# Scratch blocks in DRAM with rows of 4352 bytes in place of contiguous rows

## The chip, the core and the metric

The kernel runs on one core of a Trainium2 chip. A core has a matrix engine (PE, with its weight loads shown as PEld), a vector engine (DVE), a scalar engine (ACT), a general engine (POOL) and a synchronisation engine (SP), each with its own instruction queue, and 16 DMA engines that move data between DRAM and the on-chip memory SBUF. A DMA is issued by SP (queue q1 of the profile) or by POOL (queue q0), is cut into packets, and is spread over the DMA engines; it has landed when the last of them is done. The metric is device time in microseconds of one execution.

## The reference

Two computations share the layer-normalised input `xn` and are summed with the input. In one, a recurrent attention, segments of 32 rows are worked one after the other; each takes 8 rows of memory from the segment before:

```
for s in range(64):                       # 2048 rows, 32 per segment
    h = concat([mem, xn[32*s : 32*s+32]]) # 40 rows x 1024
    q, k, v = h @ Wq, h @ Wk, h @ Wv      # 32 heads of 128, so 4096 columns each
    p = softmax(mask(q @ k.T * scale))
    o = (p @ v) @ Wo                      # 4096 -> 1024
    mem = o[:8];  out[32*s : 32*s+32] = o[8:]
```

In the other, the two rows with the largest router value `xn @ w_r` go through one gated expert (1024 to 3584 and back), are scaled by the sigmoid of that value, and are added to their rows. The result is `x + attention + (xn + expert update)`. All tensors are bf16.

## The kernel before

**Granules.** The weights Wq, Wk, Wv and Wo, 32 MB in all, are cut into 64 granules of 128 partitions x 2048 elements, 512 KB each. Granules 0 to 47 are a slice of 128 rows by half of the columns of Wq, Wk or Wv, so a row is 4096 bytes and rows in the input lie 8192 bytes apart. Granules 48 to 63 are two slices of 128 rows of Wo, 2048 bytes a row. All 64 are needed in each of the 64 segments, in order, and not all fit in SBUF: 43 are loaded once and stay (`wres`), 21 are *streamed* (1, 4, 7, 10, 13, 16, 19, 22 and so on to 62, about one in three). Granule 10 is kept whole in on-chip accumulator memory and copied from there (`kept_piece`), and of granule 19 a quarter is kept, so that 1536 of its 2048 elements a row are streamed.

**The ring.** A streamed granule goes into one of `N_SLOT = 5` SBUF slots (`wstream`, the tile `g`). `fetch` (lines 304 to 314) issues the load on SP's queue. It is called from `after(s, g)` when a streamed granule has been used, so the next load waits for a slot whose readers on PE are done. In the first segment the load reads the inputs (line 311). From the second on it reads a scratch block in DRAM, `wsc[g]` (line 313):

```
wsc = {g: dram.tile([P, 1536 if g == KEPT_PART else 2048], ...)}      # line 103
nc.sync.dma_start(out=t[:, 0:n], in_=wsc[g][:, 0:n])                  # line 313
```

`copy_block` (lines 333 to 337) fills each `wsc` block once, during the first segment, by a DMA from the input to the scratch block on POOL's queue, in granule order, one with every second granule that is used. A block is contiguous: 128 rows of 4096 bytes one behind the other (3072 bytes in the block of granule 19). It belongs to the scratch pool `dram`, in which also `ql_d` lies, a store for queries, keys and values of the rows that a segment does not need at once.

**The segment.** Six passes multiply the segment's transposed rows with the granules (lines 614 and 597: Q, K, Q, K, V, V halves), with the attention's steps hooked in between; then Wo's 16 granules are multiplied (line 662), and the new memory goes back into the next segment's operand. Other DMAs of a segment are small ones on POOL's queue: rows of x, the stores to `ql_d` and from it, and the output rows.

**The end.** After the last segment the expert's weights are loaded (`fetch_moe`, lines 354 and 357, tiles `MW`), straight from the inputs: gate and up in rows of 3584 bytes, 7168 bytes apart, down in rows of 2048 bytes.

The order of the instructions is the program's own; no scheduler moves them.

Of the kernel before, what the change touches and what calls it, by code (L numbers as in the profile page):

```python
# [8 lines left out]
BF16 = mybir.dt.bfloat16  # L9
# [10 lines left out]
KEPT_WHOLE = 10  # L20
KEPT_PART = 19
# [6 lines left out]
def kernel(  # L28
# [16 lines left out]
    nc = tc.nc  # L45
    P = 128
# [27 lines left out]
    streamed = sorted(set(((2 * i + 1) * NG) // (2 * n_str) for i in range(n_str)))  # L74
    resident = [g for g in range(NG) if g not in streamed]

    def granule_dram(g):
        if g < 48:
            p, kc = divmod(g, KC)
            mat, half = PHASES[p]  # L80
            return Wqkv[mat][kc * P:(kc + 1) * P, 2048 * half:2048 * (half + 1)]
        w = g - 48
        return Wo2[2 * w * P:(2 * w + 2) * P, :].rearrange("(hh e) d -> e hh d", hh=2)

    def granule_out(t, g):
        return t[:, :] if g < 48 else t.rearrange("p (hh d) -> p hh d", hh=2)
# [3 lines left out]
    dram = ctx.enter_context(tc.tile_pool(name="dram", bufs=1, space=DRAM))  # L90
# [9 lines left out]


    ql_d = [dram.tile([4, P, 512], BF16, name=f"ql_d{t}") for t in range(NT)]
    wsc = {g: dram.tile([P, 1536 if g == KEPT_PART else 2048], BF16, name=f"wsc{g}") for g in streamed if g != KEPT_WHOLE}
    r_d = dram.tile([1, S], BF16, name="r_d")

    res_tiles = {}
# [55 lines left out]
    for s in range(4):  # L162
        nc.vector.tensor_copy(out=SELM[:, s, :, 0:XM],
                              in_=IDENT[:, 32 * s:32 * s + XM].unsqueeze(1).to_broadcast([P, 4, XM]))
        nc.vector.tensor_copy(out=SELL[:, s, :, :],
                              in_=IDENT.rearrange("p (s c) -> p s c", c=32)[:, :, XM:SEG])
# [166 lines left out]
    def copy_block(g):  # L333
        n = kept_at.get(g, 2048)
        if n:
            src = granule_dram(g)
            nc.gpsimd.dma_start(out=granule_out(wsc[g], g) if g >= 48 else wsc[g][:, :], in_=src if g >= 48 else src[:, 0:n])

    to_copy = list(streamed)
    flow += [(s, g) for s in range(NSEG) for g in streamed]  # L340
# [70 lines left out]
    def after(s, g):  # L411

        if s == 0:
            if g in side:
                side[g]()
            if g % 2 == 1 and g >= 8 and to_copy:
                copy_block(to_copy.pop(0))
            if n_x_left and g % 2 == 1:
                load_x(n_x_left.pop(0))
            while todo_res and todo_res[0] <= g + 2 * 64 // n_str + 8 and (todo_res[0] < resident[-10] or g >= 2 * NT + 12):  # L420
                load_resident(todo_res.pop(0))
        if g in streamed:
            fetch()
        if s == NSEG - 1:
            if g in resident:
                free_homes.append(g)
            if not flow:
                fetch_moe()
# [39 lines left out]
    for s in range(NSEG):  # L468
# [132 lines left out]
        for p, (mat, half) in enumerate(PHASES):  # L601
# [8 lines left out]
            for kc in range(KC):  # L610
                g = 8 * p + kc
# [16 lines left out]
            if mat < 2:  # L628
# [3 lines left out]
                if PSl is not None:  # L632
# [3 lines left out]
                    for jq in range(4):  # L636
                        nc.gpsimd.dma_start(out=ql_d[left[mat]][:, 32 * jq + c0:32 * jq + c0 + 8, :],  # L637
                                            in_=XBl[32 * jq:32 * jq + 32, :])
# [195 lines left out]
```

## Time and profile before

| | |
|---|---|
| median of 3 runs | 2194.16 us (2191.17 to 2204.95) |
| the profiled execution's own time | 2187.56 us |
| its span, first to last instruction | 2186.0 us |
| PE busy | 1710.7 us, 78% |
| DMA moved | 754.63 MB, mean 345 GB/s |
| `g<-wsc`: reads of a scratch block | 1197 of 512 KB and 63 of 384 KB |
| PE waiting for `g<-wsc` at line 614 | 174.0 us in 289 waits |
| mean granted PE clock | 0.94 |

The profile is one execution, taken by the hardware profiler. A row of the windows view has a stretch, the busy time of each engine (with the number of instructions), the granted PE clock, the busy share of the 16 DMA engines and the rate. [...] "To landing" is the time from the issue of a DMA to its last byte, and holds the waiting behind earlier DMAs of the same queue. The chain that ended last goes back from the last instruction to what released it, and so on. The trace holds one record for each DMA packet with its queue, size, start and duration, but not its engine.

### The profile page before, as it was taken

What the parts mean: (1) busy time and instruction counts of PE and PEld (TensorE: products, weight loads), DVE (VectorE), ACT (ScalarE), POOL (GpSimd) and SP (SyncE); (2) the same over time, 40 slices, a digit from 0 to 9 for tenths busy, and PEclk for the clock granted to TensorE, in tenths of its full rate; (3) what the DMA queues carried; (4) which work ended last, traced back from release to release, by engine and by line L of the source; (5) the groups of instructions that cost most, each with busy time, mean ns of one, the idle gap of its engine ahead of it and who ended that gap; (6) DMA issues with size and microseconds to landing.
All of it is one profiled execution on the core that took longest, in us unless ns stands there. A gap on an engine that the chain in (4) does not pass through costs nothing.

```text
span 2186.0 us, 82770 instructions
## 1 busy us (share of the span) xinstructions
PE 1710.7 (78%) x36135; PEld 907.9 (42%) x36135; DVE 718.1 (33%) x2335; ACT 670.5 (31%) x1865; POOL 641.5 (29%) x1218
## 2 busy tenths in 40 slices
PE   3257788888888788878888788888888888888854
PEld 1124444444444444444444444444444444444433
DVE  5623332332333233332333233233333333333320
ACT  0013233332333333333333333333333333333320
POOL 4223233232323322332323322332332233232120
PEclk8669999999999999999999999999999999999986
DMA  9999899998999999999999989899998999999996
GB/s 362 374 263 350 320 355 327 358 364 297 360 345 370 344 350 369 333 358 322 369 350 361 325 329 375 324 349 335 362 351 330 380 343 349 338 360 346 378 396 241
DMA packets 245244, 754.63 MB, mean 345 GB/s; under 512 B 49872, under 2 KB 56176, under 8 KB 244880
## 3 DMA queue, kind: packets, MB, share of 16 engines
q1 hardware_dynamic: 203440, 712.46, 87.5%
q0 software_dynamic: 41440, 36.86, 5.8%
q8 instruction: 283, 4.64, 0.9%
q14 instruction: 81, 0.66, 0.1%
HBM read 736.39 MB, written 22.95 MB: 347 GB/s over the span
## 4 chain that ended last, share of the span: by engine, by line
DMA 53%; PE 30%; issue 6%; ACT 4%; POOL 4%; DVE 2%; SPq 0%; ACTq 0%; DVEq 0%; POOLq 0%
DMA g<-wsc 36%; PE PSm L614 10%; DMA ql_d<-XBl 8%; PE WO L662 8%; DMA XL<-in_A_x_dram 3%; PE PSl L597 3%; PE WL L662 3%; POOL ql_d L637 2%; PE BO L550 1%; DMA LX<-ql_d 1%; POOL XL L272 1%; ACT VM L642 1%; DMA XP<-in_A_x_dram 1%; PE BT L251 1%; PE BT L484 1%
## 5 line engine op out<-in xcount | busy, mean ns | idle before, releaser
L614 PE MATMUL PSm<-wres,ST 128*32 128x512 bf16 x8192 | 683.6, 389 | 5.4 <-DVE ST L266 5.4
L614 PEld LDWEIGHTS <-ST 128*32 128x32 bf16 x12288 | 323.9, 96 | 595.3 <-issue 262.5
L614 PE MATMUL PSm<-g,ST 128*32 128x512 bf16 x4096 | 413.3, 390 | 190.6 <-DMA g<-wsc 174.0
L630 ACT CAST XB<-PSm 128x512 bf16<-128x512 f32 x256 | 150.0, 586 | 429.5 <-PE PSm L614 427.4
L637 POOL DMA_DIRECT2D ql_d<-XBl x256 | 152.4, 601 | 383.9 <-ACT XBl L634 369.8
L662 PE MATMUL WO<-wres,OT 128*32 128x256 bf16 x5632 | 254.1, 288 | 7.8 <-issue 7.6
L662 PEld LDWEIGHTS <-OT 128*32 128x32 bf16 x8192 | 206.7, 101 | 88.0 <-issue 56.9
L238 POOL DMA_DIRECT2D X<-in_A_x_dram x256 | 132.4, 525 | 375.3 <-PE WO L648 276.8
L707 POOL DMA_DIRECT2D out_dram<-OB x256 | 128.0, 507 | 383.9 <-DVE OB L705 378.3
L597 PE MATMUL PSl<-wres,STL 128*32 128x512 bf16 x2048 | 194.8, 395 | 1.7 <-ACT VL L644 1.7
L662 PE MATMUL WO<-g,OT 128*32 128x256 bf16 x2560 | 138.1, 292 | 33.2 <-DMA g<-wsc 21.7
L642 ACT CAST VM<-PSm 128x512 bf16<-128x512 f32 x128 | 76.9, 601 | 282.0 <-PE PSm L614 235.6
L557 ACT CAST OT<-BO 128x128 bf16<-128x128 f32 x256 | 67.9, 265 | 240.1 <-PE BT L552 236.6
L557 DVE CAST OT<-BT 128x128 bf16<-128x128 f32 x128 | 37.3, 291 | 315.5 <-PE BT L552 315.5
L550 PE MATMUL BO<-PT,VM 32*128 32x40 bf16 x1024 | 93.5, 180 | 42.0 <-ACT VM L642 38.6
L550 PEld LDWEIGHTS <-VM 32*128 32x128 bf16 x2048 | 65.8, 92 | 117.7 <-ACT VM L642 62.2
L519 DVE TENSOR_REDUCE NM<-BS 128x8 f32<-128x320 f32 x128 | 62.9, 491 | 153.3 <-PE BS L514 153.3
L494 DVE COPY KT<-BT 128x512 bf16<-128x512 bf16 x128 | 54.1, 422 | 171.1 <-PE BT L484 167.2
L497 DVE COPY KT<-QKL 128x128 bf16<-128x128 bf16 x128 | 24.5, 192 | 260.0 <-ACT QKL L452 260.0
L597 PEld LDWEIGHTS <-STL 128*32 128x32 bf16 x3072 | 82.4, 99 | 63.8 <-issue 17.7
L597 PE MATMUL PSl<-g,STL 128*32 128x512 bf16 x1024 | 103.7, 390 | 0.5 <-issue 0.4
L484 PE MATMUL BT<-IDENT,XB 128*128 128x128 bf16 x1024 | 102.9, 224 | 0.0
(149 smaller groups left out, 2293.7 us busy)
## 6 DMA issues: line engine op xcount, KB each, us to landing
g<-wsc SPq DMA_DIRECT2D x1197, 512.0 KB, 6.2
g<-wsc SPq DMA_DIRECT2D x63, 384.0 KB, 5.0
ql_d<-XBl POOLq DMA_DIRECT2D x256, 32.0 KB, 5.8
LX<-ql_d POOLq DMA_DIRECT2D x63, 128.0 KB, 5.4
MW<-in_B_w_gate_dram SPq DMA_DIRECT2D x16, 448.0 KB, 9.4
MW<-in_B_w_up_dram SPq DMA_DIRECT2D x16, 448.0 KB, 9.0
wres<-in_A_Wk_dram SPq DMA_DIRECT2D x12, 512.0 KB, 12.7
wres<-in_A_Wo_dram SPq DMA_DIRECT2D x11, 512.0 KB, 15.9
```

The source lines that it names most:

```text
L238: nc.gpsimd.dma_start(out=X[s % 2][32 * g:32 * g + XM, :], in_=x2[s * SEG:s * SEG + XM, 256 * g:256 * (g + 1)])
L484: nc.tensor.transpose(out=PTq[:, il, :, :].rearrange("p j r -> p (j r)"), in_=XB[:, il * P:(il + 1) * P], identity=IDENT[:, :])
L519: nc.vector.tensor_reduce(out=NM[:, :], in_=S8, axis=AX.X, op=ALU.max, negate=True)
L550: nc.tensor.matmul(o, lhsT=VM[half][q0:q0 + 32, il * P:(il + 1) * P], rhs=PTm[q0:q0 + 32, il, 0:NK], start=True, stop=False, tile_position ...
L557: copy(out=OT[half][:, 2 * ph + jl, :, :], in_=ov[:, :, 0:SEG])
L597: nc.tensor.matmul(PSl[32 * jq:32 * jq + 32, :], lhsT=STL[:, g % KC, :], rhs=Gv[:, 512 * jq:512 * (jq + 1)], start=first_, stop=last_, til ...
L614: nc.tensor.matmul(PSm[32 * jq:32 * jq + 32, :], lhsT=ST[:, kc, :], rhs=Gv[:, 512 * jq:512 * (jq + 1)], start=(kc == 0), stop=(kc == KC - ...
L630: nc.scalar.copy(out=XB[:, :], in_=PSm[:, :])
L637: nc.gpsimd.dma_start(out=ql_d[left[mat]][:, 32 * jq + c0:32 * jq + c0 + 8, :], in_=XBl[32 * jq:32 * jq + 32, :])
L642: nc.scalar.copy(out=VM[half][:, :], in_=PSm[:, :])
L662: nc.tensor.matmul(PS[32 * g:32 * g + 32, 0:256], lhsT=lhs(h), rhs=Gv[:, D * hs + 256 * g:D * hs + 256 * (g + 1)], start=False, stop=(last ...
L707: nc.gpsimd.dma_start(out=out2[s * SEG:s * SEG + XM, 256 * g:256 * (g + 1)], in_=OB[32 * g:32 * g + XM, :])
```

## The change

Every scratch block gets rows of 2048 + 128 elements, 4352 bytes, of which the first 4096 (3072 for granule 19) are written and read. Packets, bytes moved, slots, and the order and the waits of all instructions stay as they are; the addresses of the rows change, and the blocks take 544 KB of DRAM each, so each begins 544 KB behind the one before it.

```diff
-    wsc = {g: dram.tile([P, 1536 if g == KEPT_PART else 2048], BF16, name=f"wsc{g}") for g in streamed if g != KEPT_WHOLE}
+    wsc = {g: dram.tile([P, 2048 + 128], BF16, name=f"wsc{g}") for g in streamed if g != KEPT_WHOLE}
...
-            nc.gpsimd.dma_start(out=granule_out(wsc[g], g) if g >= 48 else wsc[g][:, :], in_=src if g >= 48 else src[:, 0:n])
+            nc.gpsimd.dma_start(out=granule_out(wsc[g][:, 0:2048], g) if g >= 48 else wsc[g][:, 0:n], in_=src if g >= 48 else src[:, 0:n])
```

## The prediction

> **What bounds the kernel now.** I read the page first: the busy shares, the slices, the chain that ended last. Then I cut the run into stretches with the windows view, and went to SP's waits and the DMA issues.
>
> ```profile
> span 2186.0 us, 82770 instructions
> ...
> PE 1710.7 (78%) x36135; PEld 907.9 (42%) x36135; DVE 718.1 (33%) x2335; ACT 670.5 (31%) x1865; POOL 641.5 (29%) x1218
> ...
> q1 hardware_dynamic: 203440, 712.46, 87.5%
> ...
> DMA 53%; PE 30%; issue 6%; ACT 4%; POOL 4%; DVE 2%; SPq 0%; ACTq 0%; DVEq 0%; POOLq 0%
> ```
>
> No compute engine is full, and more than half of the chain that ended last is DMA. One queue, SP's (q1), holds 87.5% of the time of all 16 DMA engines. The windows view has the streaming from the scratch blocks `wsc` as one stretch, 142 to 2105 us (the last two numbers of its row are the DMA share and GB/s):
>
> ```profile
> 142.00:2105.00 1963.00, 1629.00 (x34646) 861.47 (x34646) 638.10 (x2131) 647.91 (x1810) 587.10 (x1103) 0.97 0.95 348
> ```
>
> The DMA view of 2105 to 2150 us shows the expert weights, which come last:
>
> ```profile
> DMA packets 6337, 18.09 MB, mean 402 GB/s; under 512 B 992, under 2 KB 1040, under 8 KB 6329
> ```
>
> Streaming runs the DMA at 0.95 for 1963 us and gets 348 GB/s; the expert weights, rows of 3584 bytes at a distance of 7168, get 402. So the reads the change touches set the pace of 90% of the span, and something takes about a seventh of the rate in the streaming stage. The question is whether that something is the row distance.
>
> ```profile
> SPq L313 <- DMA g<-wsc: 482.6, 708, 4.2
> SPq L313 <- PE PSm L614: 400.9, 604, 5.1
> ```
>
> The DMA issues, with their median time to landing at the end of the line:
>
> ```profile
> g<-wsc SPq DMA_DIRECT2D x1197, 512.0 KB, 6.2
> g<-wsc SPq DMA_DIRECT2D x63, 384.0 KB, 5.0
> ...
> MW<-in_B_w_gate_dram SPq DMA_DIRECT2D x16, 448.0 KB, 9.4
> ```
>
> By the two waits, SP often waits before it issues the next block, for an earlier block to land or for PE to free a slot: the five-slot ring runs dry at times, and engines restart from idle. The expert weights are issued further ahead (9.4 us to landing against 6.2).
>
> The trace also holds one record per DMA packet. On q1 the median duration is 84 ns for 2048 bytes, 121 for 3072, 140 for 3584, 159 for 4096: a line of 9 ns plus 0.0366 ns per byte, whatever the row distance (3072 and 4096 in `wsc`, 7168 in the expert weights, 8192 in Wq, Wk, Wv). In the streaming stage the 4096-byte packets average 174 ns, with a median still at 159. I followed packets that begin within 4 ns of another's end. A packet after a data packet averages 166 ns, the first of a DMA behind the semaphore write of the one before 187, and one with no packet directly before it 216. So about two thirds of the excess over 159 (1457 of 2237 us of engine time) is in beginnings.
>
> **The change, part by part.**
>
> *Bytes and packets.* 1260 reads of 128 rows, 161,280 packets, before and after; the 256 spare bytes of a row are never moved. Cost nothing. PE, slots, waits and the order of issue stay.
>
> *Issue on SP.* A read of contiguous rows costs 320 ns of issue, one with spaced rows 328 (the views of the tiles `g` and `MW`, minimum, median and maximum in ns):
>
> ```profile
> L313 SPq DMA_DIRECT2D g<-wsc x1260: 319/320/2042, 141.8 to 2104.8; - x180
> ```
> ```profile
> L354 SPq DMA_DIRECT2D MW<-in_B_w_gate_dram x16: 327/328/650, 2105.1 to 2120.2; - x16
> ```
>
> 1260 x 8 ns = 10 us of SP's queue. On the path lie only blocks that the chain walks through: 4 in 900 to 960 us, near 2.1 a segment, 133 in 63 segments, so +1 us. The rest is hidden while SP waits for slots; without that cover it is the 10 us.
>
> *The copies into `wsc`.* 20 POOL DMAs in setup; their destination becomes spaced. They are issued up to 140 us in granule order, and land in 8 to 17 us (medians). The first is read at 142 us, and the last (granule 62) is not read until near the end of the segment that starts there, more than 20 us later. That hides them; if it did not, one late landing of some 10 us would show once. Taken as 0.
>
> *The rows, inside a block.* Rows begin 4352 bytes apart, so 15 of 16 no longer begin on a multiple of 4096 and every second one is not on a multiple of 512. For the first there is a row: the expert weights begin on multiples of 512, three quarters of them cross a multiple of 4096, and their 140 ns is the line's own value; their packets, followed in the same way, average 141 to 144. From the third packet of a DMA on, streaming packets average 161 to 163. Both are 1 to 4 ns above the line, so I take 0. Below nothing, the packets behind a data packet could lose the 6.7 ns they have over 159: 117,026 x 6.7 / 16 = 49 us. For the rows off the 512 grid there is no row; the upper end is that each moves one more piece of 512 bytes, 18.7 ns: 80,640 x 18.7 / 16 = 94 us. I stay near the expert weights' row, the nearest.
>
> *The beginnings.* Sixteen engines that restart together read rows 16 KB apart, after the change 17 KB. At 908.56 us, after a dry spell, eight engines start within 120 ns and their first packets take 424 to 987 ns, with no small DMA about. That could be a collision on addresses; it could as well be the price of any restart. The lower end is that all excess of beginnings goes: 1457 / 16 = 91 us. The upper end is more of the same, 91 us again. For no effect speak the kept-part blocks, whose rows lie 3072 bytes apart: restarts on them (157 to 347 ns in five cases) look like those on 4096. I take 0, and keep both ends.
>
> A rule bears on this. The Trainium skill, "DMA: Bandwidth & Descriptors", section "Latency and other measured facts", reports that copies slow down at row pitches of 2 MiB and more, that +4 KiB of padding restores them and +192 B does not, and that contiguous tiles are as good as padded ones. By it the blocks have no aliasing to cure and the sum is 2194. The trace's 402 against 348 GB/s would, read alone as an effect of pitch, give the faster rival below. The same page, section "How a descriptor splits into AXI transactions", cuts a descriptor that starts on 256 bytes into pieces of 256 with nothing extra; no run here has such rows.
>
> *From DMA time to span.* A saved microsecond of all 16 engines is worth at most 0.95 us, their share, and at least 0.4, since `g<-wsc` is 36% of the chain of the whole span. I use 0.7.
>
> *Sum.* +1 us and several zeros, on a profiled time of 2187.56 us (span 2186.0 and 1.6 around it). The median of the runs is 2194.16, 0.3% above. Between the two I say **2190 us**.
>
> **The rivals.**
>
> *Faster: the restarts collide on addresses, and 17 KB apart they don't.* 91 us x 0.7 = 64 us, 2130 us; with all in-block excess too, 140 x 0.7 = 98, 2096. For it: engines that restart together finish first packets late and together; the expert weights, at an uneven distance, show almost no tail. Against it: the expert weights never restart from dry, and setup reads at a distance of 8192, as even as it can be, have bunches (44.7 to 46 us, eight or more starts in 120 ns) that all take 159 ns. Excess also follows the schedule: the largest comes where PE is slow to free slots.
>
> *Slower: rows off the 512 grid cost an extra piece, each time.* 94 x 0.7 = 66 us, 2260 us; at 0.95 it is 2284. It decides (over 1%, 22 us) from 3.1 ns a packet on the average: 161,280 x 3.1 / 16 x 0.7 = 22 us. For it: the stage is at a DMA share of 0.95, so any price per packet passes through. Against it: the median packet sits on the line in every layout of this trace. No row excludes it.
>
> *The change does nothing to the memory's view*, if the mapping scatters addresses anyway. That is the forecast by another road, 2194 us.
>
> **How the numbers follow.** Forecast (within 1%, about what a measurement of this kernel can tell from no change): 0.40. Faster rival: 0.32. Slower rival: 0.28. The first has the stronger sign in the trace; the second needs less to bite. The range takes in both rivals at 0.7 and most of the way to their ends: 2115 to 2275 us. The forecast's own range is 2172 to 2216.
>
> **What would show it.** Right: `g<-wsc` to landing stays near 6.2 us, the stretch of 1963 us stays at 348 GB/s, the median packet at 159 ns, first packets near 187 and 216. SP's issue of line 313 goes from 320 to 328 ns. The faster rival shows as first packets near 165 with the median unchanged, and fewer of PE's 174 us of waits on `g<-wsc`. The slower one shows as a median above 159, or two kinds of packets, odd and even rows, and landings beyond 6.5 us. The prediction is wrong if either per-packet effect exists; the trace of before has no row at a distance off the 512 grid that could say so.

## The result, and the profile after

The changed kernel takes 2206.03 us (median, 2192.96 to 2216.01) against 2194.95 us of the kernel before, measured beside it. The ratio is **1.0047, 95% interval 1.0027 to 1.0066**: slower, by about half of the 1% that I had taken for what a measurement of this kernel can tell from no change; the interval shows that 0.2% can be told. The time lies inside the range and in the likeliest case ("within 1%"), but on the other side of no change than the 2190 us I named.

The page of the changed kernel, the lines that answer to those shown before:

```profile
span 2208.5 us, 82770 instructions
...
PE 1720.1 (78%) x36135; PEld 911.5 (41%) x36135; DVE 718.3 (33%) x2335; ACT 671.2 (30%) x1865; POOL 643.1 (29%) x1218
...
q1 hardware_dynamic: 203440, 712.46, 87.5%
...
DMA 51%; PE 31%; issue 7%; ACT 4%; POOL 4%; DVE 2%; ACTq 0%; DVEq 0%; POOLq 0%; SPq 0%
...
g<-wsc SPq DMA_DIRECT2D x1197, 512.0 KB, 6.3
g<-wsc SPq DMA_DIRECT2D x63, 384.0 KB, 4.9
```

The packets, bytes and share of SP's queue are the same to the digit. The windows view of the streaming stretch (last two numbers: DMA share, GB/s), and SP's wait and issue:

```profile
142.00:2105.00 1963.00, 1618.48 (x34317) 856.17 (x34317) 628.83 (x2101) 641.21 (x1793) 583.94 (x1094) 0.96 0.95 344
```
```profile
SPq L313 <- DMA g<-wsc: 480.6, 694, 3.4
SPq L313 <- PE PSm L614: 401.6, 595, 4.2
```
```profile
L313 SPq DMA_DIRECT2D g<-wsc x1260: 319/320/1515, 140.0 to 2126.5; - x180
```

PE's waits for a block at lines 614 and 662, first in the kernel before, then in the changed one:

```profile
PE PSm L614 <- DMA g<-wsc: 174.0, 289, 2.5
PE WO L662 <- DMA g<-wsc: 21.7, 39, 1.3
```
```profile
PE PSm L614 <- DMA g<-wsc: 167.7, 270, 2.2
PE WO L662 <- DMA g<-wsc: 26.7, 43, 1.4
```

The stretch runs at 344 GB/s in place of 348, at the same DMA share. SP's issue is still 320 ns. In the packet records the median packet is still 159 ns. What differs is the tail: a packet with none directly before it averages 224.6 ns (215.8 before), one behind a semaphore write (a packet of 4 bytes, of which the trace has 16 for each DMA of SP's queue) 195.2 (187.1), one behind a data packet 166.6 (165.7). "Before it" means on SP's queue, and is found by times alone, since the records name no engine; so some of the pairs are chance. With the packets of all queues counted, some 8,000 to 9,000 of the 21,000 of the first class have none before them, at about 260 ns in the kernel before and 282 in the changed one. Between the first and the last read of granule 19, the time of the large q1 packets above the median of their size, summed and divided by 16 engines, is 173.9 us against 152.8. I call this sum **the excess** below.

One more thing is needed to read what follows: how far two profiles of one kernel differ. The kernel before, profiled again (`e_before_null`, `j_before_null2`), gave these rows of the same stretch:

```profile
142.00:2105.00 1963.00, 1625.77 (x34395) 857.54 (x34394) 630.92 (x2106) 641.59 (x1798) 587.09 (x1103) 0.96 0.94 345
```
```profile
142.00:2105.00 1963.00, 1630.98 (x34541) 862.99 (x34533) 634.97 (x2120) 646.70 (x1805) 589.18 (x1103) 0.96 0.94 347
```

345 and 347 GB/s, at a share of 0.94, and four more profiles of the changed kernel have 345 to 350: the 348 against 344 says nothing. Landings are 6.3 and 6.3 us there, so 6.2 against 6.3 says nothing either. Nor do PE's waits for blocks, taken together, show a rise. At line 614 they are 162 to 174 us in three profiles of the kernel before and 161 to 170 in five of the changed one; at line 662 they are 20 to 22 and 24 to 27. With the waits of PE's weight loads they sum to 249 to 267 before and 246 to 262 after. Single executions of the kernel before take 2180 to 2223 us, and a per cent lower clock goes with about 15 us more (within a kernel, over all runs): the granted clock falls to half for pieces of 3.4 us or small multiples of it, 28 to 39 times in the streaming stage in the profiles of these two kernels. Single executions can't be compared to better than a per cent; only many executions can.

### The profile page after: what moved, and what is told of

Its sections match the earlier page's. It is cut to its first block, busy times and chain, and to the rows that moved or that the text cites. A ratio compares the mean times of both kernels' runs of the same rounds, so it can differ in the third digit from the quotient of the medians.

```text
span 2208.5 us, 82770 instructions
## 1 busy us (share of the span) xinstructions
PE 1720.1 (78%) x36135; PEld 911.5 (41%) x36135; DVE 718.3 (33%) x2335; ACT 671.2 (30%) x1865; POOL 643.1 (29%) x1218
## 3 DMA queue, kind: packets, MB, share of 16 engines
q1 hardware_dynamic: 203440, 712.46, 87.5%
## 4 chain that ended last, share of the span: by engine, by line
DMA 51%; PE 31%; issue 7%; ACT 4%; POOL 4%; DVE 2%; ACTq 0%; DVEq 0%; POOLq 0%; SPq 0%
DMA g<-wsc 36%; PE PSm L614 11%; DMA ql_d<-XBl 8%; PE WO L662 8%; PE PSl L597 4%; DMA XL<-in_A_x_dram 3%; PE WL L662 3%; POOL ql_d L637 2%; PE BO L550 1%; DMA LX<-ql_d 1%; ACT VM L642 1%; PE BT L251 1%; POOL XL L272 1%; PE BT L484 1%; ACT XBl L634 1%
## 5 line engine op out<-in xcount | busy, mean ns | idle before, releaser
L597 PEld LDWEIGHTS <-STL 128*32 128x32 bf16 x3072 | 82.5, 99 | 63.8 <-issue 17.5
```

The source lines that it names most:

```text
L597: nc.tensor.matmul(PSl[32 * jq:32 * jq + 32, :], lhsT=STL[:, g % KC, :], rhs=Gv[:, 512 * jq:512 * (jq + 1)], start=first_, stop=last_, til ...
```

## The experiments

Ratios are to the kernel before, run on the same chip, with 95% intervals. Diffs are against the changed kernel, unless said otherwise.

**Is it real?** The kernel before as a kernel of its own, and the changed kernel four more times, no edit in either. In the expectations, theory 1 is that the distance of the rows lengthens the beginnings, theory 2 that the distance of the blocks does, and theory 3 that nothing does.

> The kernel before, unchanged, as a kernel of its own: what the comparison gives for no change, and a second profile. Theory 1 (rows lengthen the beginnings): its packets with none directly before them average about 216 ns again, and its excess over the median packet, summed over the streaming stage and divided by 16 engines, is near 153 us, against 169 to 179 us in the changed kernel and the three others with moved addresses. Theory 3 (the profile of before was a low draw, the excess varies from run to run): 224 ns and 170 us, and the 153 us said nothing. The ratio is 1.000 within its interval.

> The changed kernel itself, for a second profile and beside the others. All theories: 1.005 of the kernel before (its 20 runs gave 1.0047, 1.0027 to 1.0066). Packets with none directly before them again average about 225 ns against 216, packets behind a semaphore write 195 against 187, the median packet 159 ns. If its beginnings come out at 216 and 187 this time, the difference between the two profiles was chance and says nothing on the cause.

> The changed kernel once more. Theory 1: 1.004 (between 1.0047 and 1.0020, the two comparisons so far). Theory 3 (no effect of the rows; the spread is that of the granted clock, which falls to half for pieces of 3.4 us when PE starves): the ratio goes along with the mean clock of its runs: 1.000 where its clock equals that of the runs of before, and about 1 us more for each 0.0005 that it is lower.

> The changed kernel, a fourth comparison. Theory 1 (a small real cost of the rows): 1.003 to 1.005 again. Theory 3 (no effect of the rows; the 1.0047 was a draw): within 0.002 of 1, as in the two comparisons since (1.0020 and 1.0014).

> The kernel before as a kernel of its own, beside the fourth comparison. Ratio 1.000 (0.9995 the first time). Excess of its packets over the median in the streaming stage, divided by 16 engines: theory 1 150 to 163 us, below all profiles of moved addresses but one (167 to 179); theory 3 anywhere between 150 and 180.

> The changed kernel, beside the two that have one part of it each. 1.0034 by the pooled comparisons (1.001 to 1.006 with this run's own uncertainty).

| | ratio | interval | excess, us | no packet before, ns | behind semaphore, ns |
|---|---|---|---|---|---|
| before, profile shown at first | | | 152.8 | 215.8 | 187.1 |
| `e_before_null` | 0.9995 | 0.9965 to 1.0024 | 162.4 | 220.2 | 190.1 |
| `j_before_null2` | 0.9989 | 0.9952 to 1.0026 | 153.9 | 213.5 | 188.4 |
| changed, the result | 1.0047 | 1.0027 to 1.0066 | 173.9 | 224.6 | 195.2 |
| `a_after_again` | 1.0020 | 0.9994 to 1.0046 | 170.1 | 224.8 | 194.6 |
| `f_after_third` | 1.0014 | 0.9982 to 1.0046 | 177.1 | 228.2 | 195.7 |
| `i_after_fourth` | 1.0040 | 1.0005 to 1.0074 | 172.6 | 222.6 | 194.7 |
| `m_after_fifth` | 1.0022 | 0.9995 to 1.0050 | 175.9 | 226.7 | 194.3 |

The five ratios, weighted by their intervals, give 1.0032, 1.0020 to 1.0043: 7 us. The four repeats without the result give 1.0023, 1.0008 to 1.0038. (The intervals are taken as independent, though comparisons on one chip share their runs of the kernel before.) The excess of the changed kernel (170 to 177, mean 173.9) doesn't touch that of the kernel before (153 to 162, mean 156.4). So both are there: 0.2 to 0.4% of time, and 17.5 us of all engines, most of it in longer beginnings. Theory 3, no effect at all, falls. That the second makes the first isn't shown by this. What `f_after_third` said of the clock is half of a story: the changed kernel's groups of runs have a mean clock of 0.9337 to 0.9352, those of the kernel before 0.9359 to 0.9379, and 0.002 of clock goes with about 3 us. Whether the lower clock is a cause or follows from more starving of PE isn't separated here.

**The rows or the distance of the blocks?** The changed kernel moves both: rows go from 4096 to 4352 bytes apart, and blocks from 512 to 544 KB (by the sizes of the tiles; the traces hold no addresses). One part alone, each twice. Blocks alone:

```diff
-    wsc = {g: dram.tile([P, 2048 + 128], ...)}
+    wsc_big = {g: dram.tile([P + 8, 2048], ...)}
+    wsc = {g: t[0:P, :] for g, t in wsc_big.items()}
```

> Rows contiguous at 4096 bytes as before, but each block is followed by 32 KB that nothing uses, so the blocks begin 544 KB apart as in the changed kernel. Theory 1 (the distance of the rows inside a block makes the beginnings slower): 1.000, beginnings 216 and 187 ns. Theory 2 (the distance between successive blocks, which overlap in flight, does it): 1.005, beginnings 225 and 195 ns.

> Contiguous rows, blocks 544 KB apart, a second time. If the block distance costs the 0.3%: 1.003. If not: 1.000 again. If both one-part kernels stay at 1.000, the loss needs both together, or is too small to be split.

Rows alone:

```diff
-    wsc = {g: dram.tile([P, 2048 + 128], ...)}
+    wsc_big = {g: dram.tile([512, 1024], ...)}
+    wsc = {g: t.rearrange("a b -> (a b)")[0:P * 2176].rearrange("(p c) -> p c", c=2176) for g, t in wsc_big.items()}
```

> Rows of 4352 bytes as in the changed kernel, but the blocks begin 1 MB apart, a power of two as before. Theory 1 (rows): 1.005, beginnings 225 and 195 ns. Theory 2 (blocks): 1.000, beginnings 216 and 187 ns.

> Rows of 4352 bytes, blocks 1 MB apart, a second time. If the rows cost the 0.3%: 1.003, and the mean of both times above 1.001. If they don't: 1.000 or below again (0.9991 the first time), and the mean of both below 1.001.

Blocks alone gave 1.0000 (0.9973 to 1.0028) and 1.0018 (0.9991 to 1.0045), with excesses of 169.0 and 165.0 us. Rows alone gave 0.9991 (0.9963 to 1.0018) and 1.0026 (0.9995 to 1.0057), with 178.9 and 170.0 us. Weighted, that is 1.0009 +- 0.0019 and 1.0006 +- 0.0021: each interval holds 1 and overlaps that of the whole change (1.0020 to 1.0043). The excess went up with either part; that it went up more with the rows is within the 4 and 9 us by which the two profiles of a part differ. The 0.3% can't be split, and this stays open.

**Other row distances.** The tile is `[P, 2048 + 64]` for 4224 bytes, `+ 256` for 4608, `+ 1024` for 6144, and `[P, 4096]` for 8192. The rows of 6144 were run after the other three, with 12 runs; those of 8192 have 6.

> Rows of 4224 bytes, 4096 + 128: every second row begins off the grid of 256 as well. The slower rival of the prediction (rows off a grid cost an extra piece), one step finer: the median packet goes above 159 ns on odd rows; with one more piece of 256 bytes, 9 ns, on 80,640 packets, 45 us of all engines, at 0.7 about 32 us or 1.015. If no grid matters down to 128 bytes: median 159 ns, 1.000 to 1.005. The Trainium skill, DMA: Bandwidth & Descriptors, section How a descriptor splits into AXI transactions, is for the first.

> Rows of 4608 bytes, so every row begins on a multiple of 512 but 15 of 16... here 7 of 8 not on a multiple of 4096; engines begin 18 KB apart, blocks 576 KB. If it is the rows off the grid of 512: 1.000. If it is that rows leave the grid of 4096, or that engines begin at 17 or 18 KB: 1.005 or more, since the engines' first addresses move by 2 KB in place of 1. Theory 2 has no number for 576 KB and says only that it needn't equal before.

> Rows of 6144 bytes (engines begin 24 KB apart, blocks 768 KB). If the loss grows with the distance: between those of 4608 (0.9987) and 8192 (1.0217), about 1.010, with packets behind a data packet near 169 ns (166 and 172 there). If 8192 is special as a power of two: 1.000 and 166 ns.

> Rows 8192 bytes apart, blocks of 1 MB: the distance that the weights have in the inputs. If the distance of rows has any hold on the beginnings, sixteen times the added distance (4096 more bytes in place of 256) shows it: 1.01 or more, or 0.99 or less, and the mean of packets with none directly before them outside 215 to 229 ns. If it has none: 1.000 within the interval, 215 to 229 ns.

| rows, bytes apart | ratio | interval | excess, us | behind a data packet, ns |
|---|---|---|---|---|
| 4224 | 0.9987 | 0.9952 to 1.0023 | 167.3 | 167.0 |
| 4608 | 0.9987 | 0.9960 to 1.0014 | 172.8 | 166.6 |
| 6144 | 1.0027 | 1.0004 to 1.0050 | 164.8 | 166.6 |
| 8192 | 1.0217 | 1.0173 to 1.0261 | 202.8 | 172.2 |

Three things follow. No grid makes itself felt: with rows of 4224 every second row begins off a multiple of 256, and the median packet is 159 ns, the 90th percentile 172, as before. The rule of the Trainium skill, "DMA: Bandwidth & Descriptors", section "How a descriptor splits into AXI transactions", by which such a start costs an extra transaction, shows in no duration here. Second, up to 6144 bytes the time doesn't follow the distance. Third, rows of 8192 cost 47 us, and not at the beginnings: a packet with none before it is at 214.7 ns, as in the kernel before, but a packet behind a data packet is at 172.2 against 166. The waits of PE, and SP's wait for an earlier block, in the kernel with rows of 8192:

```profile
PE PSm L614 <- DMA g<-wsc: 195.6, 321, 2.5
```
```profile
SPq L313 <- DMA g<-wsc: 564.2, 770, 3.4
```
```profile
g<-wsc SPq DMA_DIRECT2D x1197, 512.0 KB, 6.5
g<-wsc SPq DMA_DIRECT2D x63, 384.0 KB, 5.4
```

The kernel before has 174.0 and 482.6 us there. All waits of PE and its weight loads for blocks sum to 314 us, against 249 to 267 in the three profiles of the kernel before: here the loss does show in the waits. The stretch of 142 to 2105 us runs at 338 GB/s, against 344 to 350 in every profile of the other distances. The order and the bytes are the same, and only addresses differ, so addresses do matter, for this distance. The blocks begin 1 MB apart here, but so they do in the two kernels with rows alone, which lose nothing like it.

**Is it the power of two?** The 8192 padded by the 256 bytes of the change, `[P, 4096 + 128]`, and by 4096, `[P, 4096 + 2048]`.

> Rows of 8192 + 256 bytes: the padding of the change on the slow distance. If the power of two makes 8192 slow and 256 bytes are enough to leave it: 1.003 or less, packets behind a data packet at 166 to 167 ns. If 256 bytes are too little, or the distance itself is what costs: 1.02 and 172 ns.

> Rows of 8192 + 4096 bytes. If the distance itself costs: above 1.0217, packets behind a data packet above 172 ns. If the power of two costs: 1.003 or less and 166 to 167 ns. The Trainium skill, DMA: Bandwidth & Descriptors, section Latency and other measured facts, has a padding of 4 KB restore the rate at row pitches of megabytes, and one of 192 bytes not; carried over to 8192, it would be 1.02 for the rows of 8448 and 1.00 here.

Rows of 8448: 1.0013 (0.9988 to 1.0038), 166.6 ns behind a data packet. Rows of 12288: 1.0031 (1.0002 to 1.0060), 165.7 ns. The wait of SP with rows of 8448, and its stretch:

```profile
SPq L313 <- DMA g<-wsc: 467.4, 701, 2.9
SPq L313 <- PE PSm L614: 404.1, 608, 6.3
```
```profile
142.00:2105.00 1963.00, 1635.07 (x34524) 862.30 (x34524) 635.21 (x2121) 645.77 (x1804) 586.49 (x1103) 0.96 0.95 347
```

So it is not how far the rows lie apart. 8192 is special, and the very 256 bytes that buy nothing on 4096 buy back nearly all of the 47 us there. By the figures in the Trainium skill, "DMA: Bandwidth & Descriptors", section "Latency and other measured facts", which are for copies at a pitch of 4 MiB, a padding of 192 bytes didn't help and 4 KB did. At 8192 the paddings of 256 and of 4096 bytes both help. Why 8192 and not 4096, 4608 or 6144 isn't settled by these runs, nor whether a larger power of two would cost as much.

One thing speaks against an easy account of the 0.3%. Nine comparisons above moved the rows or the blocks in another way than the change, the rows of 8192 aside: blocks alone, rows alone, and rows of 4224, 4608, 6144, 8448 and 12288. Their excess is 165 to 179 us, mean 169.6, so they have three quarters of what the change added to it. Their ratios, weighted, give 1.0010, 1.0001 to 1.0019, a third of what the change added to the time. The larger excess comes with every one of these moves; the lost time doesn't follow it in proportion.

**Without scratch blocks.** Against the kernel before:

```diff
         elif n:
-            nc.sync.dma_start(out=t[:, 0:n], in_=wsc[g][:, 0:n])
+            if g >= 48:
+                nc.sync.dma_start(out=granule_out(t, g), in_=granule_dram(g))
+            else:
+                nc.sync.dma_start(out=t[:, 0:n], in_=granule_dram(g)[:, 0:n])
...
-    to_copy = list(streamed)
+    to_copy = []
```

> No scratch blocks and no copies: every segment streams the granules from the inputs, 15 of the 20 in rows of 4096 bytes at a distance of 8192 (granule 19 in 3072), 5 of Wo in rows of 2048 bytes, 256 packets of 84 ns in place of 128 of 159. The Wo packets cost 5 x 128 x 9 ns x 63 / 16 = 23 us of all engines more, at the 0.4 that the short rows gave 9 us, and setup is shorter by what the copies delay it, at most the 10 us of one landing. If the place or the distance of the rows matters nothing: 0.996 to 1.008. If contiguous scratch rows are what makes the reads fast: above 1.01.

1.0163 (1.0118 to 1.0207, 6 runs), 36 us. That is what the scratch blocks are worth, 9 us of it by the estimate above from the shorter rows of Wo. (The 0.4 in that estimate is from the short rows below, which were run before.) The packets tell the same tale: 172.2 ns behind a data packet, as with scratch rows of 8192. SP's issues, by source:

```profile
L315 SPq DMA_DIRECT2D g<-in_A_Wq_dram x378: 327/328/1722, 134.7 to 2124.9; - x189
...
L313 SPq DMA_DIRECT2D g<-in_A_Wo_dram x315: 367/368/893, 162.7 to 2142.4; - x158
```

Scratch rows 8192 apart are issued in 320 ns, input rows 8192 apart in 328. So the 8 ns are of the source, not of its spacing.

**What is DMA time worth?** Against the kernel before; the matmuls at lines 597, 614 and 662 leave out the same columns.

```diff
+    def short(g):
+        return 128 if g in streamed and g not in (7, 10, 16, 19, 32, 47) else 0
...
         elif n:
+            n -= short(g)
             nc.sync.dma_start(out=t[:, 0:n], in_=wsc[g][:, 0:n])
```

> Measures what DMA time is worth in span. From the second segment on, 15 of the 20 streamed granules are read with 3840 of the 4096 bytes of a row, and the matmuls of the last column quarter leave out the same 128 columns (the others of their four run beside them at full width, so PE's time stays). The kernel so leaves out part of the weights. 15 x 63 x 128 packets are 9.4 ns shorter: 71 us of all 16 engines. At the 0.7 of the prediction: 50 us less, 0.977. At 0.4: 28 us, 0.987. At 0.95: 67 us, 0.969.

0.9864 (0.9823 to 0.9904), 30 us less. The short packets' median is 149 ns, 10 below 159, so by their medians 120,960 x 10 / 16 = 76 us of all engines were taken away; a microsecond of these was worth 0.40 us (0.28 to 0.51). But the excess is 185.5 us here, 29 above that of the kernel before, so the engines got back only part of it: between the first and the last read of granule 19 the durations of SP's packets, summed and divided by 16, are 1682 us, against 1724 to 1734 in three profiles of the kernel before. That is 45 us less, and by this count a microsecond was worth 0.67.

```profile
PE PSm L620 <- DMA g<-wsc: 146.7, 253, 2.1
```
```profile
DMA 49%; PE 33%; issue 7%; ACT 4%; POOL 4%; DVE 2%; SPq 0%; ACTq 0%; DVEq 0%; POOLq 0%
DMA g<-wsc 32%; PE PSm L620 12%; PE WO L669 8%; DMA ql_d<-XBl 8%; PE PSl L602 4%; DMA XL<-in_A_x_dram 3%; PE WL L669 3%; POOL ql_d L643 2%; PE BO L554 2%; DMA LX<-ql_d 1%; POOL XL L272 1%; DMA out_dram<-OL 1%; ACT VM L648 1%; DMA XP<-in_A_x_dram 1%; PE BT L251 1%
```

PE's wait for blocks falls to 146.7 us (162 to 174 in the kernel before; the line has another number here). The chain's share of `g<-wsc` is 32%; it is 33 to 36% in three profiles of the kernel before, so this difference says little.

## Why the prediction was right or wrong

- *What bounds the kernel*: right, since less read time gives a shorter run, but the price of 0.7 for a microsecond is not one number. The short rows give 0.40 by the nominal cut and 0.67 by what the engines spent less; the rows of 8192 lose 47 us for 46 us of excess; the change lost 7 us with 17.5. The price weighed only on the rivals and the range: in the forecast it multiplied zeros. And the rate that the stretch lacks against the 402 GB/s of the expert weights is not a matter of the row distance: no distance tried gave more than 350.
- *Bytes and packets*: right; 203,440 packets and 712.46 MB in both.
- *Issue on SP*: wrong, harmlessly. I read "spaced rows" out of a row that differed in two things, spacing and source. Spaced scratch rows issue in 320 ns.
- *The copies*: no loss showed; not tried by itself.
- *Inside a block*: right. The median stays at 159 ns; packets behind a data packet go from 166 to 167. The expert weights, 512-aligned rows across multiples of 4096, were the right row to go by, and what they said held even off the grid of 256.
- *The beginnings, taken as 0*: this is the step that failed. They lengthen, from 214-220 to 223-228 ns with no packet before, and from 187-190 to 194-196 behind a semaphore write. With the little inside the blocks it is 17.5 us of all engines. The upper end I kept (91 us) was the right sign and five times too large. The zero came from the kept-part blocks, five restarts of 157 to 347 ns, which can't see 8 ns.
- *Whether the longer beginnings are the lost 7 us* stays open. At 0.40 they would be just 7 us, but that match is arithmetic, not proof. Rows of 4608 have an excess of 172.8 us and a ratio whose interval ends at 1.0014, where the same arithmetic wants 1.0030. The nine comparisons with other addresses have three quarters of the added excess and a third of the time. Of PE's waits for blocks only those at line 662 are longer in all five profiles of the changed kernel, by about 4 us (22.5 and 23.2 us with rows alone, 20.0 and 20.3 with blocks alone, so as in the kernel before); the sum of the waits isn't. And the rows of 8192 lose 47 us for 46 us of excess, which would be 18 us at 0.40 and 31 at 0.67. A block has landed when its slowest engine has; the blocks' landing rises there by 0.2 to 0.3 us (6.2 and 6.3 to 6.5) where the mean engine has only 46 / 1260 = 0.04 us more for each. A longer tail on one engine of a block would cost more than its share, and this fits, but no run separates it.
- *The sum*: its sign was not that of its terms. They came to +1 us; the 2190 lies below the 2194 of the kernel before because I put the base between one profiled execution and the median of three. No term stands behind that step down; with the median alone the sum would have been 2195.
- *The faster rival* (restarts collide on addresses 16 KB apart): falls. Of the distances from 4224 to 12288 bytes none had beginnings shorter than those of the kernel before; the shortest, with 8192 (214.7 ns with no packet before), are as long as there and come at the price told above.
- *The slower rival* (an extra piece per row off the grid): the sign came, the mechanism didn't. Rows off 512 and off 256 leave the median packet where it was.
- *The Trainium skill's rule on pitches* ("DMA: Bandwidth & Descriptors", section "Latency and other measured facts"): its advice for large pitches is to pad the rows or to lay the tiles out contiguously. For rows of 4096 that are contiguous already this leaves nothing to gain, and none was gained; the padding cost 0.3%. What I missed is that the four bunches of setup's reads at 8192, which took 159 ns, didn't show what 8192 costs in the streaming stage. They were a small part: from 2 to 35 us of the same profile the packets of 4096 bytes behind a data packet average 172 ns, though the records don't tell which of setup's sources they come from.

## What to carry to other kernels

Padding the rows in DRAM is worth a trial where they lie 8192 bytes apart, not where blocks are contiguous: here 8192 cost 2.2%, 256 bytes of padding took all or nearly all of that away, and the same padding on contiguous rows of 4096 cost 0.3%. Larger powers of two weren't tried. A busy share of 0.95 is not an exchange rate; cut a known amount of time from the resource, see what comes back, and look in the trace whether the resource was busy for that much less. And where a zero is taken for a term that can go both ways, ask whether the rows it rests on could have seen the size that matters.

## What was not expected of the hardware

- Row starts off multiples of 512 and of 256 bytes cost a read packet of 4096 bytes nothing that shows: the median is 159 ns with rows of 4096, 4224, 4352 and 4608.
- Of the distances tried, only 8192 lengthens packets inside a block, to 172 ns against 166, with the median still at 159: a tail, not a rate. 8448 and 12288 don't.
- The clock falls to half in pieces of 3.4 us or a small multiple, 28 to 39 of them in the streaming stage of eight profiles, differently in each. The mean clock goes along with part of the spread of up to two per cent between executions of one kernel (correlation -0.65 in either kernel); the rest has no cause here.
